# Lightning attention and a gated MLP on one core: q decayed in natural layout in all steps, the bias as a row, and a new hand-written order

## The chip, the cores and the metric

One core of a Trainium2 chip runs the whole kernel. It has five engines that run side by side, each with its own instruction queue in program order: TensorE (PE) multiplies matrices into PSUM, VectorE (DVE) and ScalarE (ACT) work on SBUF and PSUM, GpSimd (POOL) works on SBUF, and SyncE (SP) issues most DMAs. The metric is the device time of one execution in microseconds (us); less is better.

## The reference

Four sequences (b) of 768 tokens, eight heads (h) of 64 channels. Attention is linear with a decay lam per head, in blocks of 64 tokens, with a running state; its output, heads side by side, goes through a gated MLP whose gate mixes tokens.

```
for each block of 64 tokens:
    intra = (q k^T * Dmask) v              # Dmask[i,j] = lam^(i-j) for i >= j
    inter = (q * lam^(i+1)) @ kv_state
    out   = intra + inter
    kv_state = lam^64 * kv_state + (k * lam^(63-i))^T v
x = out of all heads, [4, 768, 512]
h = relu(x @ w_in)                         # 1024 columns
u, v = h[:, :512], h[:, 512:]
v_n = (v - mean) / sqrt(var + 1e-6)        # over the 512 columns
v_s = w_spatial @ v_n + b_spatial          # over the 768 tokens
out = (u * v_s) @ w_out
```

Inputs and output are float32.

## The kernel before

A step is 256 tokens of one sequence with all heads, so there are 12 steps, three to a sequence. Step n loads q, k and v (512 KB each) into one of three buffers. k is multiplied by a power of the decay that depends on the token's place in the whole sequence (`k_m`, by the table `lv`, made by one exponential of log lam times a position); q gets the inverse power. So scores need only a 0/1 mask, and the state needs no decay inside a sequence. In steps 0 to 4, q is cast (`q_c`), transposed on TensorE, and multiplied by its power while it leaves PSUM (`e_q`, with the table `lq`, made by twelve exponentials in `l_t`). From step 5 on, q is decayed before the transpose (`q_m`, by `lqn`), and k and q are transposed by DMA (`d_k`, `d_q`).

Then, per step: scores (`s_c`, two PSUM banks at a time), their mask (`m_k`), the state (`k_v`, copied out by `s_s`), the attention output (`a_v`), already transposed for the next product and copied out by `e_x` (`f_n` copies one element, which makes that wait explicit). `p_v` and `p_u` multiply it with the gate half and the other half of w_in; `e_v`, `e_u` apply relu on the way out of PSUM; `b_n`, `r_a`, `r_d` and `v_n` normalise the gate half. When a sequence's three steps are normalised, `p_w` multiplies with the transposed w_spatial (`w_t`, `e_w` make it once) on top of the bias that `g_p` has put into the bank; `g_m` multiplies by u, and `p_o`, `e_o`, `st_o` make and store the output in tiles of 128 tokens (`p_h`, `e_h`, `s_h` do it in halves).

The order is written by hand: ORDER is a text of tokens, and the kernel issues them one by one, without a scheduler. A token is name, arguments, and at its end the engine: T, D, A, P, S for TensorE, VectorE, ScalarE, GpSimd, SyncE. So `PV.1.0.1.T` is `p_v` of step 1, half 0, into bank 1; `PW.0.2.1.4.T` is `p_w` of sequence 0, column group 2, token half 1, bank 4; `WS.0.P` loads the first half of w_spatial from GpSimd's queue. Each engine works its own tokens in that order, and waits at each for what it needs. Two names matter here. `FL.k.w.b.new` multiplies a tile of ones by itself, k products of w columns into bank b; nothing reads the result. `GT.x.n` makes GpSimd copy one element of a loaded buffer, so that the load issued after it on that queue waits for the earlier one.

The engine letter passes through small helpers. Two of them say what the letters mean for a copy and for `k_m`, `q_m` and `v_n`:

```
def vec(e):
    return nc.vector if e == "D" else nc.gpsimd      # L184
```

`copy` (L176) takes A to ScalarE, D to VectorE, and all else to GpSimd. A line of the profile that names L178 or L180 is such a copy, and its tile names tell which.

Of the kernel before, what the change touches and what calls it, by code (L numbers as in the profile page):

```python
# [8 lines left out]
FP32 = mybir.dt.float32  # L9
# [19 lines left out]
MK.2.0.0.1.D FL.2.256.3.0.T SC.2.1.3.4.T MK.2.1.3.4.D EV.0.0.5.A RA.1.A BN.0.0.D RA.0.A RD.1.D LV.5.S RD.0.D
PU.1.0.6.T PU.1.1.2.T KV.2.0.T SS.2.0.A EU.1.0.6.A AV.2.0.0.1.T FN.2.0.1.D VN.0.0.D VN.0.1.D PU.0.1.3.T  # L30
EU.0.1.3.A KM.4.0.P AV.2.1.0.1.T EX.2.0.0.A EX.2.1.1.D GP.0.0.0.4.A EU.1.1.2.A GP.0.0.1.5.A PU.0.0.6.T VN.1.1.D
VN.1.0.D EU.0.0.6.D PV.2.0.3.T KM.4.1.P WO.P EV.2.0.3.A BN.2.0.D PV.2.1.0.T EV.2.1.0.A BN.2.1.D WT.0.0.1.T WT.1.0.2.T
EW.1.0.2.A EW.0.0.1.D RA.2.A RD.2.D VN.2.0.D WT.2.0.6.T EW.2.0.6.D PU.2.0.3.T GP.0.2.0.0.A PU.2.1.2.T VN.2.1.D
PW.0.0.0.4.T EU.2.0.3.A EU.2.1.2.A VC.3.A WT.1.1.1.T EW.1.1.1.A WT.2.1.6.T EW.2.1.6.A GP.0.3.0.3.D GM.0.0.0.4.D
GP.0.1.1.2.A PW.0.2.0.0.T GM.0.2.0.0.D GP.0.1.0.4.A WT.0.1.1.T EW.0.1.1.D PW.0.3.0.3.T TK.3.2.6.T EK.3.2.6.A
TQ.3.2.0.T PW.0.1.0.4.T GM.0.1.0.4.D EQ.3.2.0.D PW.0.1.1.2.T GM.0.1.1.2.D GM.0.3.0.3.D PW.0.0.1.5.T GM.0.0.1.5.D
KV.3.0.T SC.3.0.0.1.T MK.3.0.0.1.D SC.3.1.2.3.T MK.3.1.2.3.D GP.0.2.1.4.A PW.0.2.1.4.T TK.4.2.6.T QC.4.2.A
TQ.4.2.5.T EQ.4.2.5.D GM.0.2.1.4.D GP.0.3.1.0.A PW.0.3.1.0.T AV.3.0.1.2.T FN.3.1.2.D SS.3.0.A KV.3.1.T KM.5.1.P
EK.4.2.6.A SC.4.0.3.4.T GM.0.3.1.0.D KM.5.0.D DK.5.S AV.3.1.1.2.T EX.3.1.2.A EX.3.0.1.A SC.4.1.5.6.T
MK.4.1.5.6.D PO.0.2.0.T EO.0.2.0.A PO.0.4.2.T EO.0.4.2.D QM.5.1.P QM.5.0.D DQ.5.S VC.5.P PO.0.3.1.T PU.3.0.5.T  # L40
PV.3.1.6.T PV.3.0.0.T VC.4.A SS.3.1.D KV.4.0.T MK.4.0.3.4.D AV.4.0.2.3.T EV.3.0.0.D BN.3.0.D PO.0.5.4.T
EU.3.0.5.A SS.4.0.A KV.4.1.T EV.3.1.6.A BN.3.1.D LK.6.S KM.6.0.P FN.4.2.3.A AV.4.1.2.3.T EX.4.1.3.D SS.4.1.A
LV.6.S EX.4.0.2.A RA.3.A RD.3.D PO.0.1.0.T EO.0.1.0.A EO.0.3.1.A KV.5.0.T SC.5.0.5.6.T MK.5.0.5.6.D SC.5.1.2.3.T
MK.5.1.2.3.D SS.5.0.A PO.0.0.0.T EO.0.0.0.A LQ.6.S QM.6.0.P PV.4.1.1.T PV.4.0.5.T LK.7.S KM.7.0.P LQ.7.S
KM.6.1.D VN.3.0.D LQ.8.S DK.6.S EO.0.5.4.A AV.5.0.2.6.T FN.5.2.6.D PU.4.0.3.T EV.4.1.1.A EV.4.0.5.A QM.6.1.P
AV.5.1.2.6.T BN.4.0.D VC.6.A KV.6.0.T GP.1.2.0.0.D EX.5.0.2.D PU.4.1.4.T EU.4.0.3.A EX.5.1.6.A EU.4.1.4.A
VN.3.1.D BN.4.1.D PV.5.1.1.T EV.5.1.1.D RA.4.A RD.4.D BN.5.1.D PV.5.0.5.T LV.7.S EV.5.0.5.A BN.5.0.D RA.5.A
VN.4.1.D VN.4.0.D RD.5.D VN.5.0.D PU.3.1.2.T EU.3.1.2.A DQ.6.S QM.8.1.P QM.8.0.P VN.5.1.D KM.7.1.D DK.7.S
PU.5.0.3.T PU.5.1.6.T QM.7.1.D QM.7.0.D DQ.7.S PW.1.2.0.0.T EU.5.0.3.D SS.6.0.A GM.1.2.0.0.D LK.8.S LK.9.S
LV.8.S GP.1.3.1.4.A PW.1.3.1.4.T GP.1.0.0.1.A EU.5.1.6.A PW.1.0.0.1.T GM.1.3.1.4.D GM.1.0.0.1.D GP.1.0.1.5.A  # L50
PW.1.0.1.5.T GM.1.0.1.5.D GP.1.1.1.2.A PW.1.1.1.2.T SC.6.0.3.4.T MK.6.0.3.4.D SC.6.1.0.1.T MK.6.1.0.1.D
GP.1.2.1.6.A VC.7.A GP.1.3.0.5.A KV.6.1.T PW.1.3.0.5.T GM.1.3.0.5.D KM.8.1.P KM.8.0.P PW.1.2.1.6.T GP.1.1.0.3.A
SS.6.1.A PW.1.1.0.3.T GM.1.1.1.2.D GM.1.2.1.6.D AV.6.0.0.4.T FN.6.0.4.D KV.7.0.T SS.7.0.A SC.7.1.1.2.T
GM.1.1.0.3.D AV.6.1.0.4.T EX.6.1.4.A DQ.8.S SC.7.0.5.6.T DK.8.S KV.7.1.T PO.1.4.3.T EX.6.0.0.D PU.6.0.4.T
KM.9.0.P LV.9.S LQ.9.S EO.1.4.3.A SS.7.1.A QM.9.0.P MK.7.0.5.6.D EU.6.0.4.A MK.7.1.1.2.D PV.6.0.0.T LQ.10.S
LK.10.S QM.10.1.P QM.9.1.P KM.9.1.D VC.8.D EV.6.0.0.D PO.1.1.3.T EO.1.1.3.A LV.10.S PV.6.1.5.T EV.6.1.5.A
BN.6.1.D PO.1.5.6.T EO.1.5.6.A AV.7.0.1.4.T FN.7.1.4.A KV.8.0.T SS.8.0.A SC.8.0.2.3.T SC.8.1.5.6.T DK.9.S
LQ.11.S ST.0.1.S AV.7.1.1.4.T EX.7.0.1.A MK.8.0.2.3.D KM.10.0.P PU.6.1.0.T MK.8.1.5.6.D PO.1.0.1.T KM.10.1.P
QM.10.0.P EX.7.1.4.A PV.7.1.2.T VC.9.A DQ.9.S LK.11.S GP.2.2.0.3.A BN.6.0.D RA.6.A ST.0.0.S ST.1.4.S EV.7.1.2.A
AV.8.0.5.6.T KV.9.0.T PU.7.1.4.T FN.8.5.6.D AV.8.1.5.6.T SS.9.0.A KV.9.1.T GP.2.0.1.2.A EO.1.0.1.A BN.7.1.D  # L60
EU.6.1.0.D RD.6.D VN.6.0.D EU.7.1.4.A SS.9.1.A KM.11.0.P DK.10.S QM.11.1.P DQ.10.S LV.11.S ST.0.2.S EX.8.0.5.D
VN.6.1.D PO.1.2.1.T EX.8.1.6.A EO.1.2.1.A GP.2.1.0.0.D PV.7.0.4.T EV.7.0.4.A BN.7.0.D PV.8.1.5.T EV.8.1.5.A
RA.7.A BN.8.1.D RD.7.D ST.0.5.S PV.8.0.6.T EV.8.0.6.A BN.8.0.D RA.8.A PU.8.1.1.T VN.7.1.D RD.8.D VN.7.0.D
VN.8.0.D GP.2.0.0.4.A PU.8.0.5.T EU.8.0.5.A PU.7.0.6.T VN.8.1.D GP.2.2.1.5.A EU.7.0.6.A PW.2.0.1.2.T KM.11.1.P
GP.2.1.1.6.A GM.2.0.1.2.D EU.8.1.1.D PW.2.2.0.3.T GM.2.2.0.3.D GP.2.3.1.2.A PW.2.1.0.0.T GM.2.1.0.0.D
PW.2.3.1.2.T GM.2.3.1.2.D PW.2.2.1.5.T GM.2.2.1.5.D SC.9.0.0.1.T VC.10.A KV.10.0.T SS.10.0.A QM.11.0.P
MK.9.0.0.1.D SC.9.1.2.3.T GP.2.3.0.5.A DK.11.S PW.2.0.0.4.T GM.2.0.0.4.D MK.9.1.2.3.D PW.2.3.0.5.T GM.2.3.0.5.D
PW.2.1.1.6.T GM.2.1.1.6.D AV.9.0.0.1.T SC.10.0.2.3.T SC.10.1.4.5.T KV.10.1.T FN.9.0.1.D AV.9.1.0.1.T DQ.11.S
MK.10.0.2.3.D PO.2.2.6.T EO.2.2.6.D ST.1.1.S ST.2.2.S PO.2.5.2.T EX.9.1.1.A EX.9.0.0.A PV.9.0.3.T EV.9.0.3.D
MK.10.1.4.5.D EO.2.5.2.A PO.1.3.6.T EO.1.3.6.D PV.9.1.1.T EV.9.1.1.A BN.9.1.D SS.10.1.A PO.2.0.0.T EO.2.0.0.A  # L70
ST.2.0.S AV.10.0.3.4.T VC.11.P SC.11.1.5.6.T SC.11.0.1.2.T KV.11.0.T SS.11.0.D FN.10.3.4.A AV.10.1.3.4.T
ST.0.4.S EX.10.0.3.A EX.10.1.4.A PU.9.1.0.T MK.11.1.5.6.D BN.9.0.D PU.9.0.3.T MK.11.0.1.2.D PV.10.0.4.T
EV.10.0.4.A RA.9.A ST.0.3.S PO.2.3.5.T EO.2.3.5.A RD.9.D AV.11.0.1.6.T ST.1.5.S ST.2.5.S VN.9.1.D FN.11.1.6.D
PV.10.1.2.T EV.10.1.2.A EU.9.0.3.D BN.10.0.D AV.11.1.1.6.T EX.11.1.6.D ST.1.3.S ST.1.2.S BN.10.1.D VN.9.0.D
PO.2.1.4.T PU.10.0.5.T EX.11.0.1.A PV.11.1.2.T EO.2.1.4.A RA.10.A EU.9.1.0.A GP.3.3.0.3.D GP.3.3.1.6.A ST.1.0.S
EV.11.1.2.A BN.11.1.D PV.11.0.1.T EV.11.0.1.A GP.3.2.1.4.A BN.11.0.D RD.10.D VN.10.0.D RA.11.A PU.11.0.0.T
RD.11.D VN.10.1.D VN.11.0.D VN.11.1.D PU.10.1.2.T PU.11.1.1.T EU.10.1.2.A EU.11.1.1.D PW.3.2.1.4.T PW.3.3.1.6.T
GP.3.0.1.2.A PW.3.0.1.2.T ST.2.3.S GP.3.1.1.1.D GM.3.2.1.4.D EU.11.0.0.D PW.3.1.1.1.T ST.2.1.S GP.3.1.0.4.D
# [9 lines left out]
def kernel(  # L88
# [473 lines left out]
```

## Time and profile before

| | us |
|---|---|
| median of three runs | 148.29 (148.01 to 149.04) |
| the profiled execution | 148.77 |
| its span, first to last instruction | 147.1 |
| TensorE busy | 137.8 |
| VectorE busy | 113.5 |
| ScalarE busy | 83.0 |
| GpSimd busy | 46.0 |
| first product of the gate half (L424) | 23.36 |
| first product with w_spatial (L488) | 38.07 |

The span lies inside the execution's time; what is left over is start and end. Busy times overlap, since engines run side by side. Lines of the profile name a line of the code (L488), the engine, the operation, what it writes and reads, how often, and then busy time and the mean of one in ns; after the last bar stands the idle time before it and what ended it. In the rows of slices each digit is the busy share of a fortieth of the span, in tenths. The two DMA queues that matter are q1, which SyncE issues, and q0, which GpSimd issues.

### The profile page before, as it was taken

The numbers are of one execution on the slowest core, as the hardware profiler recorded it, in microseconds if no ns is written. First come the engines' busy times: TensorE is split into PE (matmuls) and PEld (weight loads), VectorE is DVE, ScalarE is ACT, GpSimd is POOL, SyncE is SP. The second block draws the span as 40 slices with busy tenths as digits, with TensorE's granted clock in tenths as the row PEclk, the third lists the DMA queues.
The fourth block names the chain that finished last, engine by engine and source line by source line (L and its number), as shares of the span: only waits on it lengthen the run. The fifth ranks groups of instructions, "written<-read, shape, count | busy, mean of one in ns | idle before, by whom it ended". The sixth has DMA issues, their size and how long they took to land.

```text
span 147.1 us, 4769 instructions
## 1 busy us (share of the span) xinstructions
PE 137.8 (94%) x2019; PEld 90.7 (62%) x2032; DVE 113.5 (77%) x216; ACT 83.0 (56%) x166; POOL 46.0 (31%) x57
## 2 busy tenths in 40 slices
PE   4899699999899999999999999999999999999990
PEld 2688576677576755556656747657665666666530
DVE  4448738989937998799999979797795899696720
ACT  3885622949775474695663458977414446742041
POOL 7594842017700090136050802680732000000000
PEclk9999999999999999999999999999999999999999
DMA  3999999999998015999988999999999388200524
GB/s 84 347 347 347 227 289 216 217 287 278 319 287 206 0 46 115 294 321 264 208 193 247 223 172 347 336 185 263 297 268 215 115 324 321 79 0 4 212 103 184
DMA packets 58376, 32.30 MB, mean 220 GB/s; under 512 B 15858, under 2 KB 55282, under 8 KB 58354
## 3 DMA queue, kind: packets, MB, share of 16 engines
q1 hardware_dynamic: 55968, 29.23, 75.0%
q0 software_dynamic: 2384, 2.75, 10.7%
q8 instruction: 16, 0.26, 0.7%
q14 instruction: 6, 0.05, 0.1%
q10 hardware_dynamic: 2, 0.00, 0.0%
HBM read 24.77 MB, written 6.29 MB: 211 GB/s over the span
## 4 chain that ended last, share of the span: by engine, by line
PE 82%; DVE 6%; ACT 4%; issue 3%; DMA 1%; POOL 1%; POOLq 0%
PE ps L488 21%; PE ps L424 13%; PE ps L499 12%; PE ps L462 11%; PE ps L269 6%; PE ps L321 4%; PE ps L399 4%; PE ps L352 4%; PE ps L369 4%; PE ps L390 2%; DVE a_sb L357 2%; DMA out_dram<-o_sb 1%; DVE st L439 1%; ACT uT L429 1%; ACT L220 1%
## 5 line engine op out<-in xcount | busy, mean ns | idle before, releaser
L488 PE MATMUL ps<-wt_sb,vn 128*128 128x384 bf16 x192 | 33.9, 326 | 0.7 <-DVE wt_sb L180 0.4
L291 POOL TENSOR_TENSOR kc<-k_in,lv 128x512 bf16<-128x512 f32 x18 | 19.3, 1082 | 41.1 <-DMA k_in<-in_k_dram 18.0
L357 DVE TENSOR_TENSOR a_sb<-ps,m 128x1024 bf16<-128x1024 f32 x24 | 28.7, 1216 | 2.7 <-PE ps L352 2.7
L488 PEld LDWEIGHTS <-vn 128*128 128x128 bf16 x192 | 18.2, 98 | 13.1 <-DVE vn L453 2.2
L462 PE MATMUL ps<-xT,win_sb 128*128 128x256 bf16 x192 | 23.5, 273 | 0.0
L424 PE MATMUL ps<-win_sb,xT 128*128 128x512 bf16 x92 | 22.6, 379 | 0.2
L499 PE MATMUL ps<-wout_sb,gT 128*128 128x512 bf16 x83 | 21.7, 380 | 0.7 <-issue 0.3
L494 DVE TENSOR_TENSOR gT<-ps,uT 128x384 bf16<-128x384 f32 x32 | 16.6, 550 | 6.3 <-PE ps L488 5.5
L462 PEld LDWEIGHTS <-win_sb 128*128 128x128 bf16 x192 | 18.1, 98 | 3.9
L439 DVE BATCH_NORM_STATS2 st<-vh 128x6 f32<-128x512 bf16 x24 | 16.4, 685 | 2.3 <-ACT vh L429 2.1
L178 ACT ACTIVATE ps<-bsp 128x384 f32<-128x384 f32 x26 | 12.5, 493 | 9.5 <-DVE gT L494 6.4
L178 ACT ACTIVATE o_sb<-ps 128x512 f32<-128x512 f32 x18 | 10.5, 596 | 10.9 <-PE ps L499 10.2
L269 PE MATMUL ps<-ones 128*128 128x256 bf16 x86 | 14.1, 312 | 2.8 <-DVE ones L265 1.5
L291 POOL TENSOR_TENSOR qc<-q_in,lqn 128x512 bf16<-128x512 f32 x11 | 11.9, 1085 | 15.3 <-DMA q_in<-in_q_dram 8.9
L429 ACT ACTIVATE vh<-ps 128x512 bf16<-128x512 f32 x19 | 11.3, 595 | 8.7 <-PE ps L424 8.7
L424 PEld LDWEIGHTS <-xT 128*128 128x128 bf16 x96 | 9.2, 98 | 9.5
L499 PEld LDWEIGHTS <-gT 128*128 128x128 bf16 x92 | 8.3, 98 | 9.1
L178 ACT ACTIVATE xT<-ps 128x512 bf16<-128x512 f32 x15 | 8.5, 595 | 7.4 <-PE ps L399 7.4
L453 DVE TENSOR_SCALAR vn<-vh,mv,rstd 128x512 bf16<-128x512 bf16 x24 | 12.2, 538 | 0.2
L269 PEld LDWEIGHTS <-ones 128*128 128x128 bf16 x86 | 8.8, 111 | 5.2 <-DVE ones L265 1.5
L178 ACT ACTIVATE s_sb<-ps 128x256 bf16<-128x256 f32 x17 | 6.4, 379 | 9.7 <-PE ps L369 9.6
L429 ACT ACTIVATE uT<-ps 128x512 bf16<-128x512 f32 x17 | 9.9, 588 | 1.7 <-PE ps L462 1.7
(72 smaller groups left out, 174.2 us busy)
## 6 DMA issues: line engine op xcount, KB each, us to landing
k_in<-in_k_dram SPq DMA_DIRECT2D x12, 512.0 KB, 6.3
q_in<-in_q_dram SPq DMA_DIRECT2D x12, 512.0 KB, 6.1
v_in<-in_v_dram SPq DMA_DIRECT2D x12, 512.0 KB, 6.2
out_dram<-o_sb SPq DMA_DIRECT2D x23, 256.0 KB, 3.1
wsp_raw<-in_moe_w_spatial_dram POOLq DMA_DIRECT2D x2, 576.0 KB, 12.0
win_sb<-in_moe_w_in_dram POOLq DMA_DIRECT2D x2, 512.0 KB, 10.0
wout_sb<-in_moe_w_out_dram POOLq DMA_DIRECT2D x1, 512.0 KB, 7.4
bsp<-in_moe_b_spatial_dram SPq DMA_DIRECT2D x1, 384.0 KB, 13.2
```

Of the source, the lines that this page charges most:

```text
L178: nc.scalar.activation(out=o, in_=i, func=AF.Copy)
L269: nc.tensor.matmul(out=bank(b)[:, 0:w], lhsT=ones[:, 0:P], rhs=ones[:, 0:w], start=(new == 1 and i == 0), stop=True, skip_group_check=True)
L291: vec(e).tensor_tensor(out=dst[n % NCA][:, u].rearrange("p u m o d -> p o (u m) d"), in0=src[n % NIN].rearrange("p (o u) m d -> p o u m d" ...
L357: nc.vector.tensor_tensor(out=a_sb[n % NA][:, i].rearrange("p o w j x -> p o w (j x)"), in0=ps[:, b0:b1 + 1:b1 - b0].rearrange("p o (w y) ...
L424: nc.tensor.matmul(out=bank(b), lhsT=x[:, slot(c, g)], rhs=win_sb[:, g, DH:DFF], start=(g == 0), stop=(g == NCH - 1))
L429: nc.scalar.activation(out=o, in_=i, func=AF.Relu)
L439: nc.vector.bn_stats(out=st6[p2][:, t], in_=vh[p2][:, t])
L453: vec(e).tensor_scalar(out=vn[p2][:, t], in0=vh[p2][:, t], scalar1=mv[p2][:, t, 0:1], scalar2=rstd[p2][:, t:t + 1], op0=ALU.subtract, op1= ...
L462: nc.tensor.matmul(out=pu[:, f2].rearrange("p (c x) -> p c x", c=2), lhsT=win_sb[:, g, f * P:(f + 1) * P], rhs=x[:, slot(0, g):slot(1, g) ...
L488: nc.tensor.matmul(out=bank(b)[:, 0:HW], lhsT=vn[bb % 2][:, s, f * P:(f + 1) * P], rhs=wt_sb[:, s, i * HW:(i + 1) * HW], start=False, stop ...
L494: nc.vector.tensor_tensor(out=gT[bb % 2][:, f, cols], in0=bank(b)[:, 0:HW], in1=uT[bb % 2][:, f, cols], op=ALU.mult)
L499: nc.tensor.matmul(out=bank(b), lhsT=gT[bb % 2][:, f, t * P:(t + 1) * P], rhs=wout_sb[:, f, :], start=(f == 0), stop=(f == NCH - 1))
```

## The change

q is decayed before its transpose in all twelve steps (`q_m`, by `lqn`), so `q_c`, `lq`, `llrow`, the position table `posq` and the twelve exponentials of `l_t` are gone, and `e_q` is a plain copy that either engine may do. The function tables of ScalarE are loaded by name: one that has ln and exp, and after the last exponential the one with the square root. b_spatial is loaded as one row, spread over the 128 partitions by a product with a row of ones, and copied to `bsp` in two halves. The mask, the small constant and the row of ones are set at separate places. And ORDER is written anew throughout.

```diff
-    def c_pos(e):
-        nc.gpsimd.iota(posqi, pattern=[[T2, NR], [1, 2], [2, P]], base=-MID, channel_multiplier=0)
-        nc.gpsimd.tensor_copy(out=posq, in_=posqi)
+    def c_tab(e, j):
+        nc.scalar.preload_act_table_set("sqrt_and_others" if j else "natural_log_exp_and_others")
...
-    def l_t(e, r):
-        for u in range(4):
-            nc.scalar.activation(out=lq[:, r, u].rearrange("p m x -> p (m x)"),
...
-    def b_sp(e):
-        nc.sync.dma_start(out=bsp, in_=moe_b_spatial.unsqueeze(0).to_broadcast((P, S)))
+    def b_r(e):
+        {"S": nc.sync, "A": nc.scalar}[e].dma_start(out=brow, in_=moe_b_spatial.unsqueeze(0))
+
+    def b_b(e, i, b):
+        nc.tensor.matmul(out=bank(b)[:, 0:HW], lhsT=one_row, rhs=brow[:, i * HW:(i + 1) * HW], start=True, stop=True)
+
+    def b_e(e, i, b):
+        copy(e, bsp[:, i * HW:(i + 1) * HW], bank(b)[:, 0:HW])
...
     def e_q(e, n, x, b):
-        nc.vector.tensor_tensor(out=qT[n % NTR][:, part(x)].rearrange("p u m x -> p (u m x)"),
-                                in0=quad(b)[:, part(x)].rearrange("p u m x -> p (u m x)"),
-                                in1=lq[:, n % NR, part(x)].rearrange("p u m x -> p (u m x)"), op=ALU.mult)
+        copy(e, qT[n % NTR][:, part(x)].rearrange("p u m x -> p (u m x)"),
+             quad(b)[:, part(x)].rearrange("p u m x -> p (u m x)"))
```

The new order by engine, cut to what the prediction speaks of (engine letters left out, "..." for tokens in between). TensorE's begins, and goes on to the first product with w_spatial:

```
FL.3.512.2.1 LB.6 FL.1.128.0.1 FL.5.512.2.0 TK.0.0.0 BB.1.2 TQ.0.0.0 TQ.0.1.4 BB.0.1 TK.1.1.0 TK.1.0.4 TK.0.1.5 TQ.1.0.6
SC.0.0.2.3 FL.4.512.4.0 TQ.1.1.4 KV.0.0 SC.0.1.5.6 SC.1.0.2.3 FL.1.128.0.0 KV.0.1 TQ.2.0.5 AV.0.0.4.6 AV.0.1.4.6 SC.1.1.2.3
TQ.2.1.1 FL.1.128.0.0 FL.1.256.0.0 TK.2.1.0 TK.2.0.5 KV.1.0 AV.1.0.2.3 SC.2.0.0.1 SC.2.1.4.5 KV.1.1 AV.1.1.2.3
PV.0.1.6 PV.1.1.1 PV.0.0.0 PV.1.0.2 KV.2.0 AV.2.0.3.4 PU.1.1.0 AV.2.1.3.4 PU.0.1.5 PV.2.0.4 TQ.3.2.0 PV.2.1.2
WT.0.0.1 PU.2.0.3 WT.1.0.4 PU.1.0.5 WT.2.0.1 PU.0.0.0 TK.3.2.5 PU.2.1.3 WT.0.1.0 WT.2.1.1 WT.1.1.5 PW.0.2.0.2 ...
... PW.3.2.0.2 PW.3.3.1.1 PO.3.1.2 PO.3.0.6 PO.3.2.0 PO.3.4.4 PO.3.3.3 PH.3.5.1.0 PH.3.5.0.2
```

GpSimd's, of all it does (v_n stands in the text with the letter A, and goes where `vec` sends it):

```
msk posk idn KM.1.0 QM.1.0 WI.0 QM.2.1 QM.2.0 GT.1.1 KM.2.0 WI.1 VC.1 VC.2 GT.2.2 WS.0 QM.3.1 WS.1 GT.2.1 QM.3.0 KM.3.0 GT.1.2
VN.1.1 VN.1.0 VN.0.1 VN.2.1 KM.4.0 KM.4.1 QM.4.0 WO VC.4 KM.5.0 QM.4.1 QM.5.0 KM.6.1 KM.6.0 QM.6.0 KM.7.0 QM.7.0 QM.7.1 QM.6.1
VN.3.0 VC.7 KM.8.1 KM.8.0 VN.4.1 QM.8.0 QM.8.1 KM.9.1 QM.9.1 QM.9.0 VC.8 KM.10.1 VC.9 KM.10.0 VC.10 KM.11.1 KM.11.0
VN.7.0 VN.6.1 VC.11 VN.9.0 VN.11.0
```

SyncE's first issues:

```
LK.0 LQ.0 BR LK.1 LQ.1 LV.0 LQ.2 LK.2 LV.1 LV.2 LQ.3 LK.3 LK.4 LV.3 LQ.4 LV.4 LK.5 LQ.5 LQ.6 LV.5 DK.5 DQ.5 LK.6 LV.6 LK.7 ...
```

The counts that change, old to new: FL 86 products of 256 columns to 12 of 512, three of 128 and one of 256; v_n on VectorE 24 to 14; q_m 14 to 24, k_m stays 24; v_c on GpSimd 3 to 8.

## The prediction

> **What bounds the kernel now.** I read the page's engine shares and its 40 slices, then the chain that ended last, the TensorE products of the first 40 us, GpSimd's timeline and waits, and the DMA queues by window.
>
> ```profile
> PE 137.8 (94%) x2019; PEld 90.7 (62%) x2032; DVE 113.5 (77%) x216; ACT 83.0 (56%) x166; POOL 46.0 (31%) x57
> PE   4899699999899999999999999999999999999990
> PE 82%; DVE 6%; ACT 4%; issue 3%; DMA 1%; POOL 1%; POOLq 0%
> L269 PE MATMUL ps<-ones 128*128 128x256 bf16 x86 | 14.1, 312 | 2.8 <-DVE ones L265 1.5 <-issue 1.2
> ```
>
> TensorE (PE) sets the end, but the fourth line says that 14.1 us of its busy time are products of ones, which compute nothing. They lie in the first 28 us. From the first spatial product (L488, at 38.07) to the last product (139.73 + 3.62 = 143.35) PE almost never stops: from 40 to 140 it is busy 98.98 of 100 us. So the kernel has a first part, bound by loads and by short chains, and a second part that is as long as its products.
>
> The second part in full-speed rows: 32 groups of p_w (30 products in 4.88 us, so 0.973 a group) are 31.1; 23 p_o and two p_h, at 0.865 for four products of 512 columns, 20.8; 18 p_v at 0.865, 15.6; 18 p_u at 0.872, 15.7; attention of steps 3 to 11 (16 s_c products 0.228, k_v 0.25, a half of a_v 0.46 or 0.22 without a state) 4.1 + 3.75 + 7.6; steps 3 and 4's transposes 1.8; three w_t 1.0. Sum 101.4. It took 143.35 - 38.07 = 105.3: 1.2 went before 40.25 (waits for wt_sb and vn), 2.7 after it (1.0 idle, the rest cadence).
>
> **The first part of the change.** Until 22 us the two orders run on similar chains. The removed second table load (1.283 us, 4.35 to 5.63) and the earlier one_row bring the first decayed k from 6.19 to about 5.2; but the loads land at 4.8 (k0), 6.3 (q0), 7.7 (k1), 9.4 (q1), 10.9, and the second half of the gate weights is the first thing PE's long products need. Its DMA, WI.0, was issued at 10.16 and landed 9.7 later. Now it stands behind two decays of step 1 that need q1: 9.4 + 1.04 = 10.4, landing 20.1 to 20.5. The score chain reaches PV.0.1 at about 20.0 by DVE's rows (k and q decays 0.69, mask copy 1.15, four masked scores at 1.15 to 1.2, evictions 0.42). So the first gate product starts at 20.5 instead of 23.36: the 13 products of ones and the waits before it go.
>
> What is late next is on GpSimd, where the order has moved two kinds of waits ahead of the weights:
>
> ```profile
> 14.65 0.76 POOL L249 DMA_DIRECT2D win_sb<-in_moe_w_in_dram  x1
> ...
> 17.61 0.78 POOL L254 DMA_DIRECT2D wsp_raw<-in_moe_w_spatial_dram  x1
> 18.41 1.06 POOL L291 TENSOR_TENSOR kc<-k_in,lv 128x512 bf16<-128x512 f32 x1
> 19.40 0.80 POOL L254 DMA_DIRECT2D wsp_raw<-in_moe_w_spatial_dram  x1
> 23.71 1.03 POOL L182 CAST vb<-v_in 128x1024 bf16<-128x1024 f32 x1 [3.51 <-DMA v_in<-in_v_dram]
> ```
>
> The last line waited for v2, the ninth load, and stood behind both halves of w_spatial. In the new order that cast (VC.2) is ahead of WS.0, and a decay that needs q3 (QM.3.1) is ahead of WS.1. Why v2 is late shows in the queues from 16 to 18 us:
>
> ```profile
> q0 software_dynamic: 275, 0.28, 82.4%
> q1 hardware_dynamic: 277, 0.14, 35.4%
> ```
>
> Columns are packets, MB, share of the engines. Alone, q1 moves 2064 packets in 3 us (two loads); while a GpSimd-issued load is under way it gets one packet per packet of q0, a fifth of its rate. v2 landed at 23.5 (12.7 after issue), with WI.0 and WI.1 both in front. Now WI.1 is issued at about 16.1 (after three decays of step 2) instead of 14.65, which leaves v2 a free stretch of 1.5 us more; I take 22.5. Then VC.2 ends at 23.55, a one-element copy 0.18 to 0.70, WS.0 at 24.0. GpSimd-issued loads landed 7.4, 9.7, 10.3, 11.0 and 13.0 after issue, the longer ones behind another of the same queue; WS.0 now has little before it: 9.7, so 33.7. WS.1: q3 at about 25, issue 26.2, landing 37 to 38.
>
> PE meanwhile: from 20.5 four p_v (24.0), k_v and a_v (24.7), PU.1.1 waits for WI.1 (16.1 + 10.3 = 26.4), and 4.4 us of products follow to the first w_spatial transpose, WT.0.0, at 30.8. It waits until 33.7. From there to PW.0.2 stand three w_t, PU.2.0, PU.1.0, PU.0.0, PU.2.1, another three w_t and step 3's k transposes: 6 x 0.334 + 4 x 0.872 + 0.445 = 5.94, so the first spatial product is at 39.6 instead of 38.07. WT.0.1, which needs WS.1, is due at 38.6: covered.
>
> **The second part of the change.** Three w_t (1.0) and step 3's transposes (0.9) have gone ahead of the first spatial product, so 99.5 us of products follow instead of 101.4. The 1.2 lost before 40.25 goes too, since the w_t evictions and the six vn come before. The 2.7 of cadence and idle I keep: going through the order bank by bank, I find PE and DVE within 0.5 us of each other at PW.0.2.1, PW.0.1.0, AV.4.0, SC.5 and PW.1.0, no worse than the old order's places. DVE's sum does not move: ten normalisations leave it (10 x 0.51 = 5.1), five q decays and two k decays (0.70 each), four bias copies, three output evictions, four states come. ScalarE loses the twelve lq exponentials (5.0) and bsp's broadcast load is now one row, two f32 products and two copies: an f32 product of 384 columns is not in the trace; between 0.33 (bf16) and 1.3 (four passes of it), near the 0.6 of the 128x8 pair, and hidden, as PE waits for decays there. q transposes are copied (0.42 DVE, 0.59 ACT) instead of multiplied (0.418): nothing. Neighbouring score banks change nothing either: the two banks of every s_c are neighbours in the old order too, so m_k keeps its 1.216. On SyncE's queue the small brow goes third and bsp's 13.2 us broadcast leaves; later the transposes by DMA keep their places behind the loads of their step, and DQ.5 (5.5 to landing before) is due about 0.3 after SC.5 could start, in the 2.7 kept.
>
> **The tail.** Before, the last product ended at 143.35, its eviction (ACT, 0.60) at 143.98, and the 256 KB store 3.1 later. Now the last tile is in halves, and its second half leaves by a 0.41 DVE copy and a 128 KB store (2.0 to landing, with five stores close ahead: up to 2.6): 2.5 to 3.1, I take 2.8 against 3.75.
>
> **The sum.** 39.6 + 99.5 + 2.7 + 2.8 = 144.6 against the span of 147.1: 2.5 less. The profiled execution took 148.77, above the median of the three runs (148.29, 148.01 to 149.04); the difference is taken from the median: **145.8**. One per cent, 1.5 us, is about what a measurement can tell from no change.
>
> **Rivals.** (B) *w_spatial is in time.* If v2 lands when its packets alone say (about 19.7: 9216 packets, q1's rate of 688 per us from 2.3 on, a fifth of it for 3.8 us), WS.0 leaves at 21.2 and lands at 30.9: no wait at WT.0.0, 2.9 less, 142.9. For it: the packet count; against it: by the same count v2 was due at 19.4 before, and landed at 23.5.
>
> (C) *w_spatial is later.* v2 at 23.5 as before, and 11.0 to landing: WS.0 from 24.9 to 35.9, 2.2 more, 148.0, no change.
>
> (D) *The normalisations wait on GpSimd; slower.* The order gives ten v_n the letter A, but v_n's engine is vector for D and gpsimd for all else, and the listing by engine shows them on GpSimd, in its queue. No row shows a tensor_scalar there: between 0.61 (cast of the same tile) and 1.54 (slowest two-operand row). VN.4.1 stands behind VC.7 and both halves of KM.8, which wait for the DMA transpose of kc (DK.6); all of PW.1 needs it. By medians (4.7 for DK) it ends within 0.1 us of when it is due. A transpose of 8.3 (the slowest) adds 3.6, and v_n at 1.54 another 0.9: 150.3. It decides from 4.0 us late. Speaking for it: GpSimd gets some 10 us more work and DVE's two-port operations already collide with it (v_n on DVE 381 ns at least, 1225 at most; L291 on DVE 680 to 1398). The Trainium skill (Advanced Engine Details and Errata, VectorE Performance Modes) says that the second Vector port is shared with GpSimd and that the two block each other. By that, each of ten normalisations could cost DVE up to 0.8 us of its own, 8 us spread over 100, and the sum would lose its slack at every place named above; the trace agrees only for single pairs.
>
> (E) *The clock falls.* Products of ones fall from 86 x 256 columns to 12 x 512 and four short ones, and PE now waits up to 2.9 us before WT.0.0. The trace's longest stop was 1.23 us, after which ten products still took 1.26 us, full speed; but at the start five took 1.07 (214 ns each) at 7.55 and 13 took 1.52 (117 ns) at 9.89, with the granted clock at 1.00 throughout. If one stop brings half speed back, up to 8.4 us at half rate cost 4.2; half of that is 2.1: 147.9. The Trainium skill (TensorE: Matmul & The Clock Gate, Part 1: The HAM clock gate) puts the idle window and the warm-up at about 3.4 us; by that the wait is just too short to trip it, and one trip would cost 1.7.
>
> **The numbers.** Forecast 0.42, B 0.14, C 0.22, D 0.12, E 0.10. Faster by over 1% (below 146.8): all of the forecast and B, 0.56. Within 1%: 0.17 of C, 0.03 of D, 0.08 of E, 0.28. Slower (above 149.8): 0.05 of C (13.0 to landing instead of 11.0), 0.09 of D, 0.02 of E, 0.16. The range is 142.9 to 149.6; below it lies a little of B, above it the slower ends of C, D and E.
>
> **What would show it.** Right: the first gate product at 20 to 21, one wait of PE near 31 to 34 for wsp_raw, the first spatial product near 39.6, PE busy 97 to 99% from 42 to 140, the last product near 141.8, its store 2.5 to 3.1 after. Wrong: vn on GpSimd as a releaser of L480's weights, waits of GpSimd for qT or kT around 60 to 66, products of 512 columns at 0.43 apart after a stop, or a first spatial product beyond 42.

## The result, and the profile after

The changed kernel takes 157.4 us (157.22 to 157.94, four runs) against 148.15 beside it (146.85 to 149.04): 1.064 times the time, 95% interval 1.055 to 1.072. The forecast was 145.8, with a range from 142.9 to 149.6. The profiled execution took 157.32, its span is 155.6. Some kernels below ran in a faster and a slower kind of execution (the one before, later: about 146 and 148.5), and of these the times given are those of the faster kind, and the ratios compare it alone.

From the page of the changed kernel: engine shares, TensorE's slices and its granted clock, the chain that ended last, and two groups.

```profile
PE 137.3 (88%) x1951; PEld 86.4 (56%) x1966; DVE 116.1 (75%) x210; ACT 71.7 (46%) x148; POOL 69.8 (45%) x69
...
PE   5899779789999995993599999999499999999990
...
PEclk9999999999999999999879999999999999999999
...
PE 50%; DMA 15%; POOL 7%; DVE 5%; issue 4%; ACT 2%; SPq 1%; POOLq 0%; DVEq 0%; ACTq 0%
...
L480 PE MATMUL ps<-wt_sb,vn 128*128 128x384 bf16 x192 | 35.4, 329 | 6.4 <-POOL vn L445 6.4
...
L445 POOL TENSOR_SCALAR vn<-vh,mv,rstd 128x512 bf16<-128x512 bf16 x10 | 21.5, 2148 | 16.7 <-DVE rstd L441 16.7
```

From the groups of the trace, the products of ones:

```profile
L267 PE MATMUL ps<-ones 128*128 128x512 bf16 (+2 forms) x15 | 6.0, 522 | 1.9 <-DVE ones L263 1.7 <-issue 0.2
```

The products of ones fell from 14.1 us to 6.0, as the order promised. But TensorE's row of slices now has holes (5 near 60 us, 3 and 5 from 70 to 78, 4 near 110) where the old one had nines, the chain has gone from 82% TensorE to 50%, and DMA and GpSimd have come into it. The group of the products with w_spatial names who opened the two longest, near 73 and 110 us: v_n on GpSimd, 2148 ns each. Before, the same products hardly waited, and v_n took a quarter of that on VectorE:

```profile
L488 PE MATMUL ps<-wt_sb,vn 128*128 128x384 bf16 x192 | 33.9, 326 | 0.7 <-DVE wt_sb L180 0.4
L453 DVE TENSOR_SCALAR vn<-vh,mv,rstd 128x512 bf16<-128x512 bf16 x24 | 12.2, 538 | 0.2
```

TensorE's waits, longest sums first (us in total, times, longest):

```profile
PE ps L480 <- POOL vn L445: 6.4, 2, 4.4
PE ps L267 <- DVE ones L263: 1.7, 1, 1.7
PE ps L361 <- ACT vb L175: 1.4, 1, 1.4
```

Against the steps of the forecast: the first gate product is at 23.41 (forecast 20.5, before 23.36); the first product with w_spatial at 40.12 (39.6, before 38.07); from there to the last product 111.8 (102.2); from there to the end 3.7 (2.8). So 9.6 of the 11.0 us by which the span misses the forecast lie in the second part. The rows account for nearly all of them: 6.4 of stops for v_n, 1.4 for a cast of v that waited for its load, and, as an experiment below measures, 1.6 of products at a lower clock behind the longest stop.

Another thing shows only in the DMA queues, here from 5 to 10 us (packets, MB, rate), the changed kernel first:

```profile
DMA packets 2879, 1.45 MB, mean 290 GB/s; under 512 B 49, under 2 KB 2878, under 8 KB 2879
```

and the kernel before:

```profile
DMA packets 3438, 1.74 MB, mean 347 GB/s; under 512 B 48, under 2 KB 3438, under 8 KB 3438
```

The same loads, alone on the queue, have lost a sixth of their rate. k1 lands at 8.7 instead of 7.8, q1 at 10.5 instead of 9.3, v0 at 12.3 instead of 10.8.

### The profile page after: what moved, and what is told of

It reads as the page before. It is cut to its first block, busy times and chain, and to the rows that moved or that the text cites. A ratio compares the mean times of both kernels' runs of the same rounds, so it can differ in the third digit from the quotient of the medians.

```text
span 155.6 us, 4615 instructions
## 1 busy us (share of the span) xinstructions
PE 137.3 (88%) x1951; PEld 86.4 (56%) x1966; DVE 116.1 (75%) x210; ACT 71.7 (46%) x148; POOL 69.8 (45%) x69
## 4 chain that ended last, share of the span: by engine, by line
PE 50%; DMA 15%; POOL 7%; DVE 5%; issue 4%; ACT 2%; SPq 1%; POOLq 0%; DVEq 0%; ACTq 0%
PE ps L480 19%; PE ps L454 9%; DMA v_in<-in_v_dram 7%; PE ps L491 7%; DMA wsp_raw<-in_moe_w_spatial_dram 6%; PE ps L416 5%; POOL vn L445 3%; PE ps L344 2%; PE ps L361 2%; POOL kc L284 2%; POOL vb L179 2%; DVE vn L445 2%; PE ps L391 2%; DMA q_in<-in_q_dram 2%; PE ps L466 1%
## 5 line engine op out<-in xcount | busy, mean ns | idle before, releaser
L480 PE MATMUL ps<-wt_sb,vn 128*128 128x384 bf16 x192 | 35.4, 329 | 6.4 <-POOL vn L445 6.4
L445 POOL TENSOR_SCALAR vn<-vh,mv,rstd 128x512 bf16<-128x512 bf16 x10 | 21.5, 2148 | 16.7 <-DVE rstd L441 16.7
L284 POOL TENSOR_TENSOR kc<-k_in,lv 128x512 bf16<-128x512 f32 x16 | 17.1, 1077 | 25.4 <-DMA k_in<-in_k_dram 17.9
L454 PE MATMUL ps<-xT,win_sb 128*128 128x256 bf16 x192 | 25.0, 279 | 0.0
L416 PE MATMUL ps<-win_sb,xT 128*128 128x512 bf16 x89 | 22.8, 379 | 0.5 <-issue 0.2
L284 POOL TENSOR_TENSOR qc<-q_in,lqn 128x512 bf16<-128x512 f32 x16 | 16.4, 1039 | 9.1 <-DMA q_in<-in_q_dram 4.9
L421 ACT ACTIVATE vh<-ps 128x512 bf16<-128x512 f32 x19 | 11.3, 594 | 12.4 <-PE ps L416 12.4
L175 ACT ACTIVATE ps<-bsp 128x384 f32<-128x384 f32 x22 | 10.6, 490 | 12.8 <-DVE gT L486 11.5
L179 POOL CAST vb<-v_in 128x1024 bf16<-128x1024 f32 x8 | 8.8, 1103 | 13.8 <-DMA v_in<-in_v_dram 6.8
L175 ACT ACTIVATE o_sb<-ps 128x512 f32<-128x512 f32 (+1 forms) x16 | 9.1, 580 | 6.9 <-PE ps L491 6.8
L344 PE MATMUL ps<-qT,kT 64*64 64x128 bf16 x384 | 10.2, 226 | 0.0
L391 PE MATMUL ps<-a_sb,vb 64*64 64x128 bf16 x384 | 10.2, 217 | 0.0
```

The source lines that it names most:

```text
L175: nc.scalar.activation(out=o, in_=i, func=AF.Copy)
L284: vec(e).tensor_tensor(out=dst[n % NCA][:, u].rearrange("p u m o d -> p o (u m) d"), in0=src[n % NIN].rearrange("p (o u) m d -> p o u m d" ...
L344: nc.tensor.matmul(out=pa[o][row(c), w, j], lhsT=kT[n % NTR][row(o), u, j, c * Q64:(c + 1) * Q64], rhs=qv(n, o, u, c), start=(w == 0 and j ...
L416: nc.tensor.matmul(out=bank(b), lhsT=x[:, slot(c, g)], rhs=win_sb[:, g, DH:DFF], start=(g == 0), stop=(g == NCH - 1))
L421: nc.scalar.activation(out=o, in_=i, func=AF.Relu)
L445: vec(e).tensor_scalar(out=vn[p2][:, t], in0=vh[p2][:, t], scalar1=mv[p2][:, t, 0:1], scalar2=rstd[p2][:, t:t + 1], op0=ALU.subtract, op1= ...
```

## Experiments: v_n's engine and place

**All ten v_n on VectorE.** `VN.x.y.A` became `VN.x.y.D`, ten times; nothing moved.

> The changed kernel with its ten v_n of the letter A given the letter D, each at the same place in the order, so that VectorE does all 24. Theory (v_n takes 2.1 us on GpSimd, stands there behind loads and decays, and so stops TensorE for 4.4 and 2.0 us, with slow products behind the first stop): both stops go, about 6.4, and the slow products, about 1.0, so 157.4 becomes 150. v_n on VectorE takes 0.4 to 0.6. Rival (VectorE is as full: in the changed kernel it has no idle time from 64 to 73 us, and two more v_n fall there): a stop of 1 to 2 us stays before PW.1.0, 152 to 153. Second rival (the stops only show lateness that comes from the loads, and another wait takes their place): 155 or more.

Measured: 154.9 (154.38 and 155.34). The two stops for v_n are gone (1.1 in three pieces is left), and yet only 2.5 us are. The second rival came nearest: other waits took the place. TensorE from 84 to 94 us by two (busy, then granted clock, DMA share, GB/s):

```profile
84.00:86.00 2.00, 2.00 (x14) 1.00 0.96 217
86.00:88.00 2.00, 1.06 (x41) 1.00 0.87 240
88.00:90.00 2.00, 0.99 (x68) 1.00 1.21 296
90.00:92.00 2.00, 1.67 (x22) 0.50 1.18 322
92.00:94.00 2.00, 2.00 (x8) 0.65 1.16 133
```

Short stops (0.7 for vh, 0.2 for gT, 1.0 for the cast of v8) left TensorE 2.05 us busy out of 4, and then the granted clock was 0.50. The cast of v8 stands on GpSimd behind three decays of step 9, the first of which had waited 3.71 for its load of k. So loads were late too, and hidden behind the stops for v_n until then.

**Still on GpSimd, but earlier in its queue.**

```diff
-RD.4.D VN.3.1.D DQ.7.S VC.7.P ... KM.8.1.P ... KM.8.0.P PU.3.0.0.T VN.4.1.A
+RD.4.D VN.3.1.D DQ.7.S VN.4.1.A VC.7.P ... KM.8.1.P ... KM.8.0.P PU.3.0.0.T
...
-KM.11.1.P KM.11.0.P DK.11.S ... RD.6.D RD.7.D VN.7.0.A ... VN.6.1.A
+... RD.6.D RD.7.D VN.6.1.A VN.7.0.A KM.11.1.P KM.11.0.P DK.11.S
```

> The changed kernel, v_n still on GpSimd at all ten places, but VN.4.1 ahead of VC.7 and KM.8 there, and VN.6.1 and VN.7.0 ahead of KM.11 (whose DMA transpose moves behind it). It tells the place in the queue from the duration. Theory, place and duration together: VN.4.1 runs from 70.3 to 72.4 with PW.1.0 due at 71.2, so the first stop falls from 4.4 to 1.2; the second pair runs from 104.3 to 108.5 and is due at 108.85, so that stop goes; the slow products go too: 157.4 - 3.2 - 2.0 - 1.0 = 151.2. Rival (what is delayed by it, KM.8 by 2.1 and KM.11 by 4.2, stops TensorE in turn): 153 to 156.

Measured: 155.8 (155.45 to 157.49). The first stop fell from 4.37 to 1.43 and the second went, as the theory said; the delayed KM.11 then made the DMA transpose late, and the scores of step 11 stopped TensorE for 1.7, as the rival said:

```profile
PE ps L344 <- DMA qT<-qc: 1.7, 1, 1.7
```

The wait of 1.0 for the cast of v8 was there as well, at 88, and the granted clock behind it was 0.64 and 0.51 in the two stretches of 2 us from there.

**On ScalarE, and in the old order on GpSimd.** ScalarE computes vh times rstd plus a bias; the second kernel is the old one with the letters of the same ten v_n changed.

```diff
+        if e == "A":
+            nc.vector.scalar_tensor_tensor(out=nmr[p2][:, t:t + 1], in0=mv[p2][:, t, 0:1], scalar=-1.0,
+                                           in1=rstd[p2][:, t:t + 1], op0=ALU.mult, op1=ALU.mult)
+            nc.scalar.activation(out=vn[p2][:, t], in_=vh[p2][:, t], func=AF.Identity,
+                                 scale=rstd[p2][:, t:t + 1], bias=nmr[p2][:, t:t + 1])
+            return
```

> The changed kernel with the ten v_n of the letter A done on ScalarE, at the same places in the order: one activation with scale rstd and a bias of minus mean times rstd, which VectorE makes by one more operation of one column. Theory: as with all on VectorE, the stops and the slow products go; 0.6 each on ScalarE, which is idle half the time: 150. Rival (ScalarE's relus and copies around them become late by 0.6 each, and the extra 0.15 on VectorE falls where it is full): 152 to 153.

> The kernel before with the same ten v_n moved to GpSimd, each at its own place in the old order; nothing else changed. Theory: 2.1 us each instead of 0.5; the old order's GpSimd is busy 31%, but v_n stands in it behind decays that wait for loads, and w_spatial's products follow v_n closely: some batches stop TensorE by 2 to 4 us, 151 to 156. Rival (the new order's crowded queue is the cause, not the engine): within 1 us of before, 148 to 149.

Measured: 154.6 (153.51 to 155.25) on ScalarE, where one v_n takes 0.81 us, not 0.6; that is under half of the expected gain. In the old order, ten v_n on GpSimd make 1.17 times the time of before (95% interval 1.13 to 1.21; 170.8 and 172.9 us), far outside what I expected, with a mean granted clock of 0.94 against 0.995 to 1.00 for the kernel before. The profiled run of it had a granted clock near 0.57 almost throughout, unlike those two, so its trace can't say which waits these were; that is left open. It does settle that the crowded new queue is not needed for the damage.

## Experiments: the rate of the loads

**The row of b_spatial as the suspect.** It is the one new DMA among the first loads. The row moves from SyncE's queue to ScalarE's (`BR.S` to `BR.A`); then that and all v_n on VectorE; then the old kernel with the row loaded as well (`LQ.0.S BR.S`), for nothing.

> The changed kernel with one letter changed: the load of b_spatial's row (768 numbers, one partition) is issued by ScalarE instead of third on SyncE's queue. Giving v_n to VectorE or ScalarE brought the time only to 155 or 156, so most of the loss is elsewhere; in all three traces SyncE's loads run at 290 GB/s from 5 us on, where the kernel before has 347. Theory (the one-row load on that queue slows every later load on it): the loads run at 347 again, the waits for v_in and for DMA transposes go, the first gate product comes at 21 to 22 instead of 23.4; v_n's stops stay: 151 to 153. Rival (the slower rate has another cause, such as the order of the loads or the missing broadcast): 290 stays, 157.

> Both: the row on ScalarE's queue and all ten v_n on VectorE. Theory (the two causes together make the loss): loads at 347, no stop over 1.5 us after 40 us, no slow products, 145 to 148, at or below before. Rival (the order itself is worse, by chains that the loads only covered): 150 or more.

> The kernel before with one DMA more: b_spatial's row is also loaded into a tile of one partition, third on SyncE's queue, and nothing reads it. Theory (a one-row load on the queue slows all that follow): the rate falls from 347 to about 290 GB/s from 5 us on; loads of k1 to v2 land 1 to 3 us later, and the first gate product moves from 23.4 to 25 or later: 150 to 153. Rival: 347 stays and the time is that of before, 148 to 149.

Measured: 157.95 (156.67 to 158.53) with 290 GB/s; 153.85 (153.39 to 154.59), 290 as well; and 146.0 for the old kernel, ratio 1.000 (0.994 to 1.006), with 347. The theory fell three times: the row costs nothing that can be measured, and is not the cause of the rate.

**Where the tiles start.** What remained was where the loads write. The change took tables away (`lq`, `posq` and others), and every tile allocated behind them moved down in SBUF. q_in, k_in and v_in start at multiples of 512 bytes in the old kernel; in the new one, at 480 above such a multiple, which is 32 above a multiple of 64. One constant made wider moves them by 32 bytes:

```diff
-    eps_t = sb([P, 1], FP32, "eps_t")
+    eps_t = sb([P, 16], FP32, "eps_t")
```

In the new kernel that puts them back on multiples of 512; in the old one it moves them off, to 32 above. The third kernel has the constant of the first and all v_n on VectorE. All large tiles behind the constant move with it, those of the weights, casts and outputs too: the rate from 5 to 10 us is that of the loads of k, q and v alone, while the times hold whatever else the move does.

> The changed kernel with one constant, eps_t, made 16 columns wide instead of one, so that every large tile behind it in SBUF starts 32 bytes later. The change took tables away, and all tiles from w_in on moved from multiples of 64 bytes (before) to 32 above such a multiple. The row on its own queue left the loads at 290 GB/s, and the old kernel with that row loaded at 347, so the row is not the cause. Theory (the start of the load buffers is the cause): loads at 347 GB/s from 5 us on, first gate product at 21 to 22 instead of 23.4, the waits for v_in shorter; v_n's stops stay: 151 to 153. Rival (the start of a tile does not matter; the rate falls by the order of the loads): 290 stays, 157.

> The kernel before with the same widening of eps_t, which there moves the large tiles from multiples of 64 bytes to 32 above. Theory (the start of the load buffers sets the rate): its loads fall from 347 to 290 GB/s, k1 to v2 land 1 to 3 us later, the first gate product comes 1 to 3 us later; behind 40 us its loads have slack: 150 to 153. Rival: 347 and 148, as before.

> The changed kernel with both repairs: tiles at multiples of 64 bytes, and all ten v_n on VectorE. Theory (these two are the loss): loads at 347, no stop over 1 us behind 40 us, no slow products there: 145 to 148, where the forecast of 145.8 was. Rival (the order itself has more waits than I found, which neither repair removes): 150 or more.

Measured, with the queue's row from 5 to 10 us of the first and of the second:

```profile
DMA packets 3433, 1.73 MB, mean 347 GB/s; under 512 B 50, under 2 KB 3432, under 8 KB 3433
```

```profile
DMA packets 2881, 1.45 MB, mean 290 GB/s; under 512 B 48, under 2 KB 2881, under 8 KB 2881
```

154.6 (153.16 to 155.03), first gate product 22.5; the old kernel moved off 150.9 (150.11 and 151.68), ratio 1.032 (1.010 to 1.053); and 151.0 (149.99 to 151.78) with both repairs, ratio to before 1.032 (1.020 to 1.044). The cause of the lower rate is shown from both sides. One detail was wrong: in the old kernel moved off, the first gate product stayed at 23.37, and the first product with w_spatial at 38.1. What stands ahead of them in the old order seems to have taken the lateness up; it came out at 111 us, as a wait of 1.8 for a DMA transpose of q, with a granted clock of 0.83 from 110 to 120.

**Which start is good enough.** The kernel with both repairs, its tiles at 64 and at 256 above a multiple of 512 (eps_t 32 and 80 columns wide), one run each.

> As the kernel with both repairs, but with the large tiles at 64 above a multiple of 512 bytes (eps_t 32 columns wide) instead of at multiples of 512. If 64 bytes are the unit: loads at 347 GB/s, 150 to 152. If the start has to be a multiple of a packet (512 bytes): 290 GB/s, 154 or more.

> The same kernel as the one with both repairs, with the large tiles at 256 above a multiple of 512 bytes (eps_t 80 columns wide). At 0 the loads ran at 347 GB/s, at 64 above at 290, as at 32 above. If a half of a packet of 512 bytes is enough: 347 GB/s and 150 to 152. If a packet has to start at a multiple of its own size: 290 GB/s, about 153.

Measured: 153.04 and 150.38. The queue from 5 to 10 us at 64 above, then at 256 above:

```profile
DMA packets 2877, 1.45 MB, mean 290 GB/s; under 512 B 49, under 2 KB 2876, under 8 KB 2877
```

```profile
DMA packets 3403, 1.72 MB, mean 344 GB/s; under 512 B 51, under 2 KB 3402, under 8 KB 3403
```

64 is not enough, 256 is; 128 wasn't tried. The Trainium skill (DMA: Bandwidth & Descriptors, How a descriptor splits into AXI transactions) says that a descriptor is split into transactions that start at 256-byte boundaries, so that one of 512 bytes which starts off such a boundary needs three instead of two and fetches bytes that it doesn't use. The traces fit that unit, though a unit of 128 would fit them too: 347 and 344 GB/s at 0 and 256, 290 at 32, 64 and 480, however many bytes would go unused. The section tells it of reading; here the end that is off is the one written.

## Experiments: what was left of the 5 us

With both repairs 151.0 was left, 5.2 above the forecast. TensorE's stops behind 40 us there (start, duration, and in brackets the wait ahead):

```profile
40.97 0.81 PE L480 MATMUL ps<-wt_sb,vn 128*128 128x384 bf16 x4 [0.59 <-DVE wt_sb L177]
42.23 0.64 PE L344 MATMUL ps<-qT,kT 64*64 64x128 bf16 x32 [0.44 <-DVE wt_sb L177]
60.91 0.44 PE L361 MATMUL ps<-vb,kc 64*64 64x64 bf16 x16 [0.29 <-ACT vb L175]
68.65 1.91 PE L454 MATMUL ps<-xT,win_sb 128*128 128x256 bf16 x16 [0.32 <-DVE uT L423]
...
78.25 0.30 PE L382 MATMUL ps<-qT,s_sb 64*64 64x128 bf16 x6 [1.32 <-issue]
```

With two of 0.2 they sum to 3.3. In the first part, the bias products and the products of ones (the changed kernel; the repaired one has the same):

```profile
6.91 1.64 PE L256 MATMUL ps<-brow,one_row 1*128 1x384 f32 x2 [0.40 <-DMA brow<-in_moe_b_spatial_dram]
8.49 1.03 PE L314 MATMUL ps<-ident,qc 128*128 128x128 bf16 x8
9.45 1.64 PE L256 MATMUL ps<-brow,one_row 1*128 1x384 f32 x2
```

Each stands ahead of transposes that the scores need. Four kernels on top of the repairs: the bias products moved to later places (`BB.0.1.T` ahead of KV.0.1, where it takes the place of a short product of ones, `BB.1.6.T` ahead of AV.2.0, with its copy on ScalarE); `FL.4.512.4.0.T` left out, whose result is not used; v_n on ScalarE instead of VectorE; and these three together.

> On top of both repairs (tiles at multiples of 64 bytes, v_n on VectorE; 151.0): the two products that spread b_spatial's row are moved from the first 10 us, where they stand ahead of q's and k's transposes, to two later places where TensorE waits. Theory (I took them as hidden, but they take 1.64 each there and hold up the score chain): the first scores come 1 to 1.5 us earlier than 12.28, the first gate product near 22 instead of 23.15, 149.5 to 150. Rival (hidden behind the loads after all): no change, 151.

> On top of both repairs (151.0): the four products of ones between the first and the second scores (FL.4.512.4.0) are left out; their result is not used. Theory (they take 1.9 us at 12.85 on the chain, ahead of a transpose that the next scores wait for): the first gate product comes about 1.5 us earlier than 23.15, 149.5. Rival (they keep TensorE fast; without them it stays at half rate longer, and the products behind take twice as long): the gain is given back, 151 to 153.

> The changed kernel with tiles at multiples of 64 bytes and the ten v_n on ScalarE (one activation each, with a one-column product on VectorE for the bias). It tells whether VectorE's load is what is left: with v_n there, evictions of the transposed w_spatial at 38 to 42 us come 1 us late and TensorE waits 1.6 in three stops. Theory (VectorE is too full for ten more): those stops go, 149.5 to 150 against 151.0. Rival (ScalarE becomes late in turn, or the stops are not what the time hangs on): 151 or more.

> All at once: tiles at multiples of 64 bytes, the ten v_n on ScalarE, the products of b_spatial's row moved later, FL.4.512.4.0 left out. If the four losses are separate and add up, 146.5 to 147.5, below before (148.3); if they cover one another, or TensorE stays at half rate longer in the first part, 148.5 to 150.

Measured: 150.25 (149.52 to 150.82), 148.3 (147.74 and 148.91), 150.97 (150.11 to 151.99) and 150.5 (149.67 to 151.58). The first gate product came at 21.8, 21.6, 22.8, and at 20.2 with all three: the forecast's 20.5 could be had, once these two were out of the chain. But it didn't carry to the end. With v_n on ScalarE the waits for evictions of wt_sb went, and two of 0.6 for ScalarE's evictions of u stood in their place, as the rival said. With all three, the first product with w_spatial is at 38.0 and the last product ends at 145.0, 106.9 later, where the old kernel takes 105.3. They cover one another: what is gained ahead is waited for behind, at w_spatial (0.95), at the cast of v8 (1.0), at v_n (0.6) and at a bias copy (0.9).

**v_n split.** With the tiles mended, the first product with w_spatial came at 38.0 where GpSimd did v_n, and at 39.9 where VectorE did, since evictions of wt_sb then queue behind v_n on VectorE. So the first sequence's four stay on GpSimd, the other six go to VectorE, with the bias products late and FL.4.512.4.0 out.

> Tiles at multiples of 64 bytes, the bias products moved later, FL.4.512.4.0 left out, and v_n split: the first sequence's four stay on GpSimd, which is idle there (28 to 34 us), the other six are VectorE's. Theory (what v_n costs hangs on the place: GpSimd idle and time to spare in the first sequence, VectorE too full at 38 to 42): no stop at the transposed w_spatial, none at PW.1.0 over 0.6, 146.5 to 148, level with before or a little below. Rival (the second part's stops move on to the next late thing): 149 to 150.5 as with the single repairs.

Measured: 150.1 (148.21 to 150.22), ratio 1.031 (1.021 to 1.041): the rival. The runs compared have a mean granted clock of 0.954 to 0.975, against 0.977 to 1.00 with both repairs alone. Its trace, of a run at 0.955, shows where the clock went: 0.50 from 10 to 20 us and 0.79 from 20 to 25, and the first gate product at 22.95, not at the 20.2 above. That the products left out at the start are the cause isn't shown: the kernel with its tiles at 256 above has them all, and reads 0.50 from 10 to 15. No version beat the kernel before.

**Is a slow product the stop's doing?** Tiles mended, v_n on GpSimd, and 16 products of ones put into the stop; their result is not used.

```diff
-PW.1.0.1.4.T
+FL.16.512.2.0.T PW.1.0.1.4.T
```

> The changed kernel with tiles at multiples of 64 bytes and v_n still on GpSimd, and 16 products of ones of 512 columns (3.5 us at full speed) put right ahead of PW.1.0.1, where TensorE stopped for 3.7 us. Theory (the stop itself makes the products behind it slow): granted clock 1.00 from 70 to 80 instead of 0.66, products of p_u at 0.27 and p_w at 0.33, 1 us gained against 0.2 to 0.5 lost by the late start of the first three products. Rival (the clock falls by a rhythm of its own): still a slice at 0.6 to 0.8 there or near it.

Measured: 151.6 in one run, against 154.6 (153.16 to 155.03) without them. TensorE by two us (busy, granted clock, DMA share, GB/s), first without the products of ones:

```profile
70.00:72.00 2.00, 0.00 (x0) 1.00 1.02 217
72.00:74.00 2.00, 1.33 (x15) 0.53 0.69 167
74.00:76.00 2.00, 2.00 (x53) 0.50 1.15 346
76.00:78.00 2.00, 2.00 (x9) 0.50 1.14 333
78.00:80.00 2.00, 2.00 (x14) 0.76 1.68 268
```

and with them:

```profile
70.00:72.00 2.00, 1.95 (x10) 1.00 1.03 221
72.00:74.00 2.00, 1.58 (x53) 1.00 1.06 307
74.00:76.00 2.00, 2.00 (x16) 1.00 1.15 347
76.00:78.00 2.00, 2.00 (x87) 1.00 1.11 329
```

The theory holds. From the first product after the wait to the attention products of step 6, the same work takes 72.67 to 79.92, 7.25 us, without and 72.51 to 76.85, 4.34, with: 2.9 us are the lower clock's. In the changed kernel the same stretch, 75.57 to 81.49, is 5.92: 1.6 more.

## Why the prediction was wrong, by its steps

Two steps carry 6.4 of the 11.6 us between 145.8 and 157.4: the rate of the loads, and the price of v_n on GpSimd. With both put right 151.0 is left, and the steps behind these two tell where the rest lies, as far as it is known.

**"The loads land at 4.8 (k0), 6.3 (q0), 7.7 (k1), 9.4 (q1)."** This is the step that no rival covered. The loads' rate was taken over from the old trace as if it belonged to the queue; it belonged to the tiles' start as well. Price: 2.8 with v_n on GpSimd (157.4 to 154.6), 2.7 and 3.9 with it on VectorE (153.04 to 150.38, 154.9 to 151.0), 4.6 in the old order (ratio 1.032).

**"Between 0.61 and 1.54" for v_n on GpSimd (rival D).** The mechanism, the place (VN.4.1 behind VC.7 and KM.8, ahead of PW.1) and the releaser were right. The term was mis-sized: 2062 ns at least, 2074 in the middle, 2720 at most, against 382 to 1277 on VectorE. Neither bounding row was the same operation on that engine. GpSimd's queue around the stop:

```profile
65.22 3.04 POOL L284 TENSOR_TENSOR qc<-q_in,lqn 128x512 bf16<-128x512 f32 x3 [1.82 <-issue]
68.25 2.07 POOL L445 TENSOR_SCALAR vn<-vh,mv,rstd 128x512 bf16<-128x512 bf16 x1
70.28 1.07 POOL L179 CAST vb<-v_in 128x1024 bf16<-128x1024 f32 x1
71.33 2.12 POOL L284 TENSOR_TENSOR kc<-k_in,lv 128x512 bf16<-128x512 f32 x2
73.44 2.07 POOL L445 TENSOR_SCALAR vn<-vh,mv,rstd 128x512 bf16<-128x512 bf16 x1
```

No wait for a DMA transpose is in it: it took no slow DK.6, as D had assumed, only work in a row. A second stop like it (2.04, VN.7.0 and VN.6.1 behind KM.11) I had not found at all. With the tiles mended, v_n's engine is worth 3.6 (154.6 to 151.0).

**Rivals D and E as alternatives.** E ("one stop brings half speed back") was given its own chance beside D. But D's stop is what brings E about, so their prices add. The Trainium skill (TensorE: Matmul & The Clock Gate, Part 1: The HAM clock gate) puts the idle window at about 3.4 us; the stops of 4.37 and 3.70 agree, and stops up to 1.3 with work around them left 1.00. But the cluster on VectorE's kernel, no single stop over 1.0, also ended at 0.50, so one whole window of idleness is not needed here. Nor does the length of a stop decide alone: the changed kernel's second, of 2.04, left 1.00, and the one of 1.83 in the old kernel moved off was followed by 0.50 from 112 to 114. What decides below 3.4 us stays open.

**"The first gate product starts at 20.5."** It came at 23.41. The chain was worked out by VectorE's rows, without what stands in TensorE's own queue: the bias products were "hidden", and at 1.64 each, above the bound of 1.3, they held the transposes up (moving them: 1.35 earlier); FL.4.512.4.0, 1.9 us between the first scores and the next, was not priced (leaving it out: 1.5 earlier). Out of both, 20.2 in one kernel, and 22.95 in the one that split v_n.

Behind both sizes stands a cost that the forecast saw in the old trace (214 ns and then 117 for a product of ones) and did not carry over to the new order: half speed at the start. Four transposes in the kernel before:

```profile
8.41 0.63 PE L321 MATMUL ps<-ident,kc 128*128 128x128 bf16 x4
11.26 0.39 PE L321 MATMUL ps<-ident,kc 128*128 128x128 bf16 x4
```

and in the changed kernel:

```profile
12.28 0.63 PE L314 MATMUL ps<-ident,qc 128*128 128x128 bf16 x4
15.04 0.39 PE L314 MATMUL ps<-ident,qc 128*128 128x128 bf16 x4
```

So TensorE still ran at the slow rate at 12.3, where the old order had the fast one by 11.3, though the granted clock reads 1.00 throughout in both. At their later places the bias products take 0.91, within the bound, where TensorE is fast. In every trace of the new order the rate that TensorE keeps through the first part comes at 13 us or later. The order's fewer products of ones may be the reason, but no run puts them back, and how much of the 2.9 it makes isn't shown.

**"WS.0 at 24.0, landing 33.7", "the first spatial product at 39.6".** WS.0 was issued at 24.33 and landed at 34.11; the product came at 40.12. The number held in part by luck: WT.0.0 waited 0.6 for it, not 2.9, because everything ahead was late as well.

**"99.5 us of products and the 2.7 I keep."** Even with both repairs, and a trace at full clock throughout, 106.4 lie between the first spatial and the last product. My walk through the banks found VectorE and TensorE "within 0.5 us of each other" at five places, and stops of 0.3 to 1.3 stand at others: VectorE is late with wt_sb once v_n is its work, ScalarE with vb. Named stops are 3.3 of the 6.9 above the products' sum; the rest is cadence, of which I had counted 1.7, and where it comes from stays open.

**"2.8" for the tail.** 3.7, no better than before. The copy of 0.42 was right; from its end to the end of the span are 3.2, where I had 2.0 to 2.6 for the store. The store of 128 KB did land 1.9 after its issue, but 1.1 follow to the end of the span, in which the engines only end the program. The old tail has the same 1.1: of its 3.1, the 256 KB store took 2.0. So half the size saved 0.1, and the 1.1 was left out of the sum.

## What to carry to other kernels

When tiles come or go, look where the load buffers behind them start: here their loads ran at 344 to 347 GB/s at a multiple of 256 bytes and at 290 off it, and no line of the diff says so. Price an operation on an engine by a row of that operation on that engine, and where there is none, take the chance of a price outside the rows seriously. A long stop of TensorE costs its length and then the slow products behind it, so rivals of which one sets off the other are added, not weighed against each other. And the time from a store's issue to the end of the span is not that of the store: the last 1.1 us are the same in both kernels.

## What the runs showed of the hardware that I had not expected

- Loads of 512-byte packets into SBUF: 347 and 344 GB/s with tiles at 0 and 256 above a multiple of 512 bytes, 290 at 32, 64 and 480 above.
- A subtract and multiply by two per-partition scalars on 128x512 bf16: 2.07 us on GpSimd in the middle and 2.06 at least, 0.41 and 0.38 on VectorE.
- After stops of 4.37 and 3.70 us the granted clock fell to 0.5 for 3.4 and 6.8 us; products of ones in the stop kept it at 1.00. Stops of 1.0, 0.7 and 0.2 close together did it too; a single one of 2.04 did not.
- A product of one row in f32, 1 x 384, takes two instructions: 1.64 us at the start of the kernel, where transposes ran at half rate too, and 0.91 later.
